# K and V loads of an attention decode step issued from GpSimd, with one packet asked for per DMA engine

## The chip, the cores and the metric

The kernel runs on one core of a Trainium2 chip. The metric is device time in microseconds (us) of one execution. The profile is one execution of the kernel as the hardware profiler records it; its span, from the first to the last instruction, is about 1.8 us shorter than the device time here.

## The reference

One decode step for four sequences: layer norm, attention over a cache of 4,096 positions with 32 heads of 192, a residual, layer norm again, and a gated feed-forward block.

```python
q = (layernorm(x) @ wq)                     # B=4, D=640 -> 32 heads x 192
scores = einsum("bhqd,bhkd->bhqk", q, k_cache) * 192 ** -0.5
o = einsum("bhqk,bhkd->bhqd", softmax(scores), v_cache)
h = x + o.reshape(B, 1, 32 * 192) @ wo
out = h + (silu(layernorm(h) @ w_gate) * (layernorm(h) @ w_up)) @ w_down
```

The K and V caches are 402.65 MB of the 424.29 MB that are read, all in bf16. Every byte is used once.

## The kernel before

The work is cut into 32 units, four heads of one sequence each. A unit needs one K tile and one V tile of 128 rows (partitions) x 49,152 bytes, 6.29 MB. There are two K slots, one V slot, and the last V goes into a free K slot. `wq` (128 rows of 61,440 bytes) shares memory with the second K slot and with V, so the second K and the first V must wait until `wq` has been used. In each unit VectorE forms four products of K and q, TensorE and VectorE sum them into scores, ScalarE takes exponentials, and TensorE forms the weighted sum of V (`pv`), one unit late.

All large loads are issued from SyncE (`sp`), in one queue:

```python
wq_land = dma("sp", lambda e: e.dma_start(wqsb..., wq...), S_wq)      # first DMA of the queue
...
def load_k(u):
    deps = [lambda: tk["tt", u - 2, NQ - 1]] if u >= 2 else ([wq_used] if u == 1 else [])
    landed["k", u] = dma("sp", lambda e: e.dma_start(
        kslot[u % 2][:, :, :].rearrange("q t d -> q (t d)"), src(kc, u)), S_k[u % 2], deps)

def load_v(u):
    if u < NU - 1:
        deps = [(lambda: tk["pv", u - 1]) if u >= 1 else wq_used]
    else:
        deps = [lambda: tk["tt", u - 1, NQ - 1]]
    landed["v", u] = dma("sp", lambda e: e.dma_start(vsrc(u)..., src(vc, u)), ..., deps)

load_k(0); load_k(1)
for u in range(NU):
    load_v(u)
    if u + 2 < NU:
        load_k(u + 2)
...   # wo in two parts (the first waits for the weighted sum of unit 30), then w_gate, w_up, w_down: all "sp"
```

`("tt", u, 3)` is the last product of unit u, `("pv", u)` the weighted sum. In a unit the fourth product is issued, then the weighted sum of the unit before. GpSimd (`pool`) only builds constants in the first 5.5 us. x is loaded from ScalarE's queue.

## Time and profile before

| | before |
|---|---|
| device time, median (range) of the first 4 runs | 989.79 us (989.71 to 990.20) |
| bytes read | 424.29 MB |
| first large DMA packet starts, last one ends (packet records) | 1.77 us, 984.75 us |
| VectorE, TensorE busy | 56%, 59% |

The first view is the page of the kernel before: the span, the busy tenths of the DMA engines and the GB/s that they moved in 40 equal slices, the queue with its packets, MB and share of 16 engines' time, the chain of work that ended last by engine, VectorE's products (busy us, mean ns | idle us before them and what ended it), and DMA issues (count, KB each, median us from issue to landing).

```profile
span 988.1 us, 9499 instructions
...
DMA  9999999999999999999999999999999999999997
GB/s 401 428 438 430 434 434 426 442 428 436 432 428 442 428 436 432 428 442 426 438 432 428 442 422 440 434 428 442 422 440 434 428 442 420 442 434 428 442 429 330
...
q1 hardware_dynamic: 10528, 424.29, 99.5%
...
DMA 67%; PE 18%; DVE 13%; issue 1%; SPq 1%; DVEq 0%
...
L412 DVE TENSOR_TENSOR prod<-k,qball 128x6144 f16<-128x6144 bf16 x128 | 426.4, 3352 | 221.1 <-DMA k<-in_A_k_cache_dram 221.1
...
k<-in_A_k_cache_dram SPq DMA_DIRECT2D x32, 6144.0 KB, 39.5
v<-in_A_v_cache_dram SPq DMA_DIRECT2D x31, 6144.0 KB, 25.5
wq_sb<-in_A_wq_dram SPq DMA_DIRECT2D x1, 7680.0 KB, 21.5
k<-in_A_v_cache_dram SPq DMA_DIRECT2D x1, 6144.0 KB, 39.5
```

The DMA engines are busy in all of the span but its last slice. The chain is two thirds DMA. VectorE sits idle 221 us for K. So the span is the stream of bytes, plus what comes before its first byte and after its last. A V lands 25.5 us after its issue, though its own transfer needs 14.5 (6.29 MB at the 433 GB/s that moved between 100 and 900 us): by that estimate about 11 us of earlier work is still queued at each issue. That is the slack an issuer has.

The second view is the timeline of the same kernel (start us, duration us, engine and line, operation; in brackets the idle time before and what ended it): the start, two pairs of issues in the steady part, and the end.

```profile
0.74 0.41 SPq L330 DMA_DIRECT2D wq_sb<-in_A_wq_dram  x1
...
22.36 0.49 PE L337 MATMUL pb<-wq_sb,lnT 128*4 128x384 bf16 x4 [12.08 <-DMA wq_sb<-in_A_wq_dram]
...
36.85 6.63 DVE L412 TENSOR_TENSOR prod<-k,qball 128x6144 f16<-128x6144 bf16 x2 [24.73 <-DMA k<-in_A_k_cache_dram]
...
855.15 0.33 SPq L365 DMA_DIRECT2D v<-in_A_v_cache_dram  x1
...
855.53 0.43 SPq L354 DMA_DIRECT2D k<-in_A_k_cache_dram  x1
...
883.35 0.33 SPq L365 DMA_DIRECT2D v<-in_A_v_cache_dram  x1
...
883.72 0.43 SPq L354 DMA_DIRECT2D k<-in_A_k_cache_dram  x1
...
941.43 3.01 SPq L376 DMA_DIRECT2D wo_sb<-in_A_wo_dram  x2
...
953.12 5.03 PE L462 MATMUL pb<-k,pbuf 128*8 128x384 bf16 x64 [3.50 <-DMA k<-in_A_v_cache_dram]
...
966.85 5.67 PE L504 MATMUL pb<-wo_sb,OT 128*4 128x160 bf16 x192 [6.50 <-DMA wo_sb<-in_A_wo_dram]
...
985.99 0.67 SPq L586 DMA_DIRECT2D out_dram<-gu  x2
```

The first product waits for the first K, 36.85 us in. V and the next K are issued together. At the end TensorE waits 3.5 us for the last V and then 6.5 us for wo.

### The profile page before, as it was taken

To read this page: it belongs to the slowest core of one execution; us is meant where nothing else is said; L and a number is where in the kernel's file an instruction comes from. 1 tells how busy PE (TensorE), PEld (TensorE's weight loads), DVE (VectorE), ACT (ScalarE), POOL (GpSimd) and SP (SyncE) were. 2 spreads that over 40 slices of the span, in tenths; PEclk is the share of its full clock that TensorE was granted. 3 is DMA by queue.
4 is the path that set the end of the run, shared out by engine and by line. 5 is a ranking of instruction groups with operands and counts; after the bars stand their busy time and mean duration, and the time that the engine had idled before them with its cause. 6 is when DMAs were issued, how large, how long until landed. Compare 5 with 4: busy or idle time off the path is not lost.

```text
span 988.1 us, 9499 instructions
## 1 busy us (share of the span) xinstructions
PE 581.9 (59%) x4422; PEld 130.3 (13%) x2955; DVE 553.4 (56%) x454; ACT 117.1 (12%) x376; POOL 3.7 (0%) x18
## 2 busy tenths in 40 slices
PE   1676454676555567556566655656665555765556
PEld 0011011111011111001111110111101011110023
DVE  2486555566655556655556665555666455566621
ACT  0311111100111110111111011111101111100120
POOL 1000000000000000000000000000000000000000
PEclk9798777887777887777788777788877778887776
DMA  9999999999999999999999999999999999999997
GB/s 401 428 438 430 434 434 426 442 428 436 432 428 442 428 436 432 428 442 426 438 432 428 442 422 440 434 428 442 422 440 434 428 442 420 442 434 428 442 429 330
DMA packets 10584, 424.40 MB, mean 430 GB/s; under 512 B 1232, under 2 KB 1232, under 8 KB 1744
## 3 DMA queue, kind: packets, MB, share of 16 engines
q1 hardware_dynamic: 10528, 424.29, 99.5%
q8 instruction: 5, 0.08, 0.0%
q14 instruction: 3, 0.02, 0.0%
q10 hardware_dynamic: 48, 0.01, 0.0%
HBM read 424.29 MB, written 0.01 MB: 429 GB/s over the span
## 4 chain that ended last, share of the span: by engine, by line
DMA 67%; PE 18%; DVE 13%; issue 1%; SPq 1%; DVEq 0%
DMA k<-in_A_k_cache_dram 64%; DVE prod L412 12%; PE pb L161 11%; PE pb L462 4%; DMA wu_sb<-in_B_w_up_dram 4%; PE pb L420 2%; SPq L365 0%; DVE sc L425 0%; PE pb L468 0%; PE pb L582 0%; DVEq L412 0%; DVE guT L576 0%; PE pb L569 0%; PE pb L560 0%; DVE gu L575 0%
## 5 line engine op out<-in xcount | busy, mean ns | idle before, releaser
L412 DVE TENSOR_TENSOR prod<-k,qball 128x6144 f16<-128x6144 bf16 x128 | 426.4, 3352 | 221.1 <-DMA k<-in_A_k_cache_dram 221.1
L161 PE MATMUL pb<-prod,identH 128*128 128x512 f16 x1408 | 384.1, 430 | 0.0
L420 PE MATMUL pb<-prod,identH 128*128 128x512 f16 x128 | 58.1, 454 | 339.9 <-DVE prod L412 339.9
L425 DVE TENSOR_REDUCE sc<-pb 128x32 f32<-128x512 f32 x128 | 88.1, 688 | 106.9 <-PE pb L161 106.9
L477 ACT ACTIVATE otmp<-pb,minv 128x192 f32<-128x192 f32 x32 | 13.4, 420 | 650.9 <-PE pb L462 650.9
L420 PEld LDWEIGHTS pb<-prod,identH 128*128 128x128 f16 x128 | 13.2, 103 | 585.9 <-DVE prod L412 485.1
L462 PE MATMUL pb<-v,pbuf 128*8 128x384 bf16 x1984 | 86.0, 326 | 0.0
L453 ACT ACTIVATE pbuf<-sc,negM 32x128 bf16<-32x128 f32 x128 | 73.4, 574 | 4.9
L462 PEld LDWEIGHTS pb<-v,pbuf 128*8 128x8 bf16 x1984 | 45.5, 87 | 28.8
L481 DVE SCALAR_TENSOR_TENSOR orow<-pb,minv,otmp 128x192 f32<-128x192 f32 x32 | 13.4, 418 | 55.2 <-ACT otmp L477 55.2
L497 PEld LDWEIGHTS pb<-orow,here 128*128 128x128 f32 x256 | 33.6, 192 | 73.5 <-issue 71.1
L497 PE MATMUL pb<-orow,here 128*128 128x48 f32 x256 | 31.7, 267 | 1.1 <-DVE orow L481 1.1
L453 ACT ACTIVATION_READ_ACCUMULATOR pbuf<-sc,negM 32x1 f32 x128 | 31.7, 248 | 0.0
L447 ACT ACTIVATE negM<-pb 128x4 f32<-128x4 f32 x32 | 5.5, 173 | 160.6 <-PE pb L443 160.6
L468 PEld LDWEIGHTS pb<-lsb,headm 128*128 128x128 f32 x64 | 12.3, 194 | 74.7 <-issue 71.1
L443 PE MATMUL pb<-negMc,ones_row 1*128 1x4 f32 x64 | 12.2, 258 | 11.9 <-DVE negMc L438 11.9
L434 PE MATMUL pb<-identF,msb 128*1 128x128 f32 x64 | 12.1, 271 | 9.8 <-DVE msb L430 9.8
L438 DVE TENSOR_REDUCE negMc<-pb 1x4 f32<-1x128 f32 x32 | 8.9, 279 | 15.1 <-PE pb L434 15.1
L443 PEld LDWEIGHTS pb<-negMc,ones_row 1*128 1x128 f32 x64 | 9.4, 183 | 21.3 <-DVE negMc L438 21.3
L468 PE MATMUL pb<-lsb,headm 128*128 128x1 f32 x64 | 9.2, 214 | 2.7 <-ACT pbuf L453 2.7
L490 ACT ACTIVATE here<-place 128x131 f32 (+1 forms) x32 | 10.0, 312 | 0.8
L430 DVE TENSOR_REDUCE msb<-sc 128x1 f32<-128x128 f32 x32 | 9.2, 286 | 1.1
(70 smaller groups left out, 89.2 us busy)
## 6 DMA issues: line engine op xcount, KB each, us to landing
k<-in_A_k_cache_dram SPq DMA_DIRECT2D x32, 6144.0 KB, 39.5
v<-in_A_v_cache_dram SPq DMA_DIRECT2D x31, 6144.0 KB, 25.5
wq_sb<-in_A_wq_dram SPq DMA_DIRECT2D x1, 7680.0 KB, 21.5
k<-in_A_v_cache_dram SPq DMA_DIRECT2D x1, 6144.0 KB, 39.5
wo_sb<-in_A_wo_dram SPq DMA_DIRECT2D x1, 5760.0 KB, 25.3
wo_sb<-in_A_wo_dram SPq DMA_DIRECT2D x1, 1920.0 KB, 27.2
wg_sb<-in_B_w_gate_dram SPq DMA_DIRECT2D x1, 1920.0 KB, 31.4
wu_sb<-in_B_w_up_dram SPq DMA_DIRECT2D x1, 1152.0 KB, 33.8
```

The costliest lines, as they stand in the source:

```text
L161: return e.add_instruction(mybir.InstMatmult(name=e.bass.get_next_instruction_name(), engine=mybir.EngineType.PE, start_tensor_calc=start, ...
L412: op("dve", lambda e: e.tensor_tensor(out=prod[BUF[k]][:, :, :], in0=kslot[u % 2][:, k * QT:(k + 1) * QT, :], in1=qball[:, bass.ds(u + pr. ...
L420: op("pe", lambda e, j=j: (e.matmul if j == 0 else partial(held_matmul, e))(psR[k][:, 0:QT * R], lhsT=identH[:, :], rhs=prod[BUF[k]][:, :, ...
L425: op("dve", lambda e: e.tensor_reduce(sc[u % 2][:, k * QT:(k + 1) * QT], psR[k][:, 0:QT * R].rearrange("q (t r) -> q t r", r=R), AX.X, ALU ...
L434: op("pe", lambda e: e.matmul(psS[0:1, XT], lhsT=msb[:, 0:1], rhs=identF[:, :], start=True, stop=True), [g("rmax", u), g("negM", u - 1), p ...
L443: op("pe", lambda e: e.matmul(psS[:, XB], lhsT=ones_row[0:1, :], rhs=negMc[0:1, :], start=True, stop=True), [g("hmax", u), g("negM", u - 1 ...
L453: op("act", lambda e, h=h, r=r: e.activation(out=pbuf[r, :, h], in_=sc[u % 2][r, :], func=ACTF.Exp, bias=negM[r, h:h + 1], scale=alpha, ac ...
L462: op("pe", lambda e, t=t, n=n: e.matmul(psO[32 * n:32 * n + 8, 0:2 * DH], lhsT=pbuf[:, t:t + 2, :].rearrange("q t m -> q (t m)"), rhs=vsrc ...
L468: op("pe", lambda e: e.matmul(psS[:, XL], lhsT=headm[:, :, :].rearrange("q r m -> q (r m)"), rhs=lsb[:, :], start=True, stop=True), [g("ex ...
L477: op("act", lambda e: e.activation(out=otmp[:, :], in_=psO[:, 0:DH], func=ACTF.Copy, scale=minv[:, 0:1]), [g("pv", u), g("minv", u), g("st ...
L481: op("dve", lambda e: e.scalar_tensor_tensor(out=orow[:, :], in0=psO[:, DH:2 * DH], scalar=minv[:, 1:2], in1=otmp[:, :], op0=ALU.mult, op1 ...
L497: op("pe", lambda e, i=i: e.matmul(psT[:, bass.ds(JW * at_unit(u)[0], JW)], lhsT=here[:, NI - 1 - i:NI - 1 - i + 128], rhs=orow[:, JW * i: ...
```

## The change

The intent, as the change reads: take the whole K and V stream, with wq ahead of it, off SyncE, let each DMA engine move its eight rows of a tile as one packet, and leave SyncE free for the weights that follow. The ending moves too: SyncE instead of GpSimd waits for the output, and GpSimd is drained at the end of the block.

```diff
+    wq_land = dma("pool", lambda e: e.dma_start(          # now ahead of the constants on GpSimd
+        wqsb..., wq...), S_wq)
     c1 = op("pool", lambda e: e.memset(r32[:, :], 0.0))
 ... (cut)
-    wq_land = dma("sp", lambda e: e.dma_start(wqsb..., wq...), S_wq)
 ... (cut)
-        landed["k", u] = dma("sp", lambda e: e.dma_start(
-            kslot[u % 2]..., src(kc, u)), S_k[u % 2], deps)
+        landed["k", u] = dma("pool", lambda e: e.dma_start(
+            kslot[u % 2]..., src(kc, u), single_packet=True), S_k[u % 2], deps)
 ... (cut)
-        landed["v", u] = dma("sp", lambda e: e.dma_start(
-            vsrc(u)..., src(vc, u)), ..., deps)
+        landed["v", u] = dma("pool", lambda e: e.dma_start(
+            vsrc(u)..., src(vc, u), single_packet=True), ..., deps)
 ... (cut; wo and the feed-forward weights stay on "sp")
-    with nc.Block(no_gpsimd_drain=True) as block:
-        pr.emit(block, "pool", fin[-1:])
+    with nc.Block() as block:
+        pr.emit(block, "sp", fin[-1:])
```

More of the change, by code (lines that the diff above doesn't have):

```diff
@@ L271, in build_kernel @@
     xd = dma("act", lambda e: e.dma_start(x16[:, :], x[:, 0, :].rearrange("b (n d) -> (b n) d", n=4)), S_x)
+    wq_land = dma("pool", lambda e: e.dma_start(
+        wqsb[:, :, :].rearrange("q c n -> q (c n)"), wq[:, :].rearrange("(q c) n -> q (c n)", c=CD)), S_wq)
     c1 = op("pool", lambda e: e.memset(r32[:, :], 0.0))
@@ L327, in build_kernel @@
     ln1 = layer_norm(psH[:, 0:DQ], [xs])
-    wq_land = dma("sp", lambda e: e.dma_start(
-        wqsb[:, :, :].rearrange("q c n -> q (c n)"), wq[:, :].rearrange("(q c) n -> q (c n)", c=CD)), S_wq)
     qcopy = []
@@ L353, in load_k @@
         deps = [lambda: tk["tt", u - 2, NQ - 1]] if u >= 2 else ([wq_used] if u == 1 else [])
-        landed["k", u] = dma("sp", lambda e: e.dma_start(
-            kslot[u % 2][:, :, :].rearrange("q t d -> q (t d)"), src(kc, u)), S_k[u % 2], deps)
+        landed["k", u] = dma("pool", lambda e: e.dma_start(
+            kslot[u % 2][:, :, :].rearrange("q t d -> q (t d)"), src(kc, u), single_packet=True), S_k[u % 2], deps)
     def vsrc(u):
@@ L364, in load_v @@
             deps = [lambda: tk["tt", u - 1, NQ - 1]]
-        landed["v", u] = dma("sp", lambda e: e.dma_start(
-            vsrc(u)[:, :, :].rearrange("q t d -> q (t d)"), src(vc, u)), S_v if u < NU - 1 else sem("s_vlast"), deps)
+        landed["v", u] = dma("pool", lambda e: e.dma_start(
+            vsrc(u)[:, :, :].rearrange("q t d -> q (t d)"), src(vc, u), single_packet=True), S_v if u < NU - 1 else sem("s_vlast"), deps)
     load_k(0)
```

## The prediction

> **What bounds the kernel now.** The DMA stream. The slice table has DMA at 9 in 39 of 40 slices; the queue table gives SyncE's queue 99.5% of all 16 engines' time. The chain of waits is 64% "DMA k". VectorE is 56% busy, TensorE 59%; the waits list has VectorE idle 221 us for K. The timeline shows SyncE issuing V and the next K in pairs, 29.04 us apart on average, right after the weighted sum of the unit before. Such a V lands 25.5 us after its issue although 6.29 MB need about 14.5 us, so about 11 us of queued work is left at each issue.
>
> **How far from its limit.** The DMA packet records show a 49,152-byte row as one packet of 1.820 us, 15,360 bytes as 0.578 us: 36.75 ns per 1,000 bytes, and some 13 ns that do not grow with size. Per transfer an engine spends 29.04/2 = 14.52 us on eight rows; by the slope alone it would be 14.45 us. The difference, 0.07 us, times 64 is 4.4 us (an estimate): all that packet merging can win.
>
> **What the change does.**
> 1. One packet of eight rows. Gain 0 to 4.4 us on the critical path; I take 3.5.
> 2. [...]VectorE's products (3.35 us each) could delay an issue, but the pair is issued after the unit's fourth product, when VectorE goes on to wait for K; even two products in a row, 6.7 us, fit into the 11 us of queued work. Cost about 0, apart from the first load: wq begins perhaps 0.7 us later, on the critical path.
> 3. The engines that move data stay the same: the rate is otherwise unchanged.
> 4. Weights now come on another queue than the last V. wo was issued at 941.4 us, when the last V had 11.7 us left. [...]wo follows it as before. Cost about 0.
> 5. [...]The records have instruction fetches at 60.8, 94 and 108 us, in mid-stream. Each might hold an engine up for one packet; less the 11 us of slack that is 0 to 3.5 us. I take 0.5 us in all.
> 6. Closing on SyncE and draining GpSimd: below 0.5 us.
>
> **Sum.** 989.85 - 3.5 + 0.7 + 0.5 = about 987.5; as the merging may be complete I say 987.0 us, 984.0 to 991.0. Faster by over 2%: 1%; within 2%: 95%; slower by over 2%: 4%.
>
> **What would show it.** Step 1: mid-stream GB/s up from 433.5 to 435, pairs 28.9 us apart. Step 2: VectorE's wait for K still about 220 us, V landing about 25 us after issue, no gaps in DMA; the first product at 37 to 38 us instead of 36.85. Step 4: last V's landing to the end still 35 us. Step 5: a single late unit near 60 to 110 us, if at all.
>
> **What would make it wrong.** [...]If packet boundaries cost nothing, step 1 gives 0 and the time is 990 to 991 us.

Cut from it, where marked, is what neither the profile of before nor a later run shows: how GpSimd's issues work inside, what could lock them out or slow single engines (step 2 and the last paragraph), why wo would follow the last V (step 4), and how long others wait for a long packet (step 5). The sum: 989.85 - 3.5 + 0.7 + 0.5 = 987.55. The 0.7 us of step 2 and the limit of 0.5 us of step 6 were guesses; experiments and profile below measure them. The 3.5 us in step 5 are an estimate, the 14.52 us of eight rows less the 11 us of slack; that a fetch waits that long was not shown. The packet records show only that each fetch in mid-stream (three in before, four in after) starts 3 to 4 ns before the record of a row ends.

## The result, and the profile after

The kernel after takes 991.20 us (median of 4 runs, 990.54 to 991.54) against 989.79 us. The ratio is 1.0013, with a 95% interval from 0.9995 to 1.0030: no difference by the 2% rule. Ratios here are the mean time of one kernel's fast runs over that of the other's fast runs of the same rounds, so they are not quite the ratio of the medians. The measured median lies 0.2 us above the predicted range, and 4.2 us above the predicted value.

The page of the kernel after, the lines that answer to those of before, with the added line of GpSimd's issues:

```profile
span 988.7 us, 9496 instructions
...
DMA  9999999999999999999999999999999999999997
GB/s 383 443 422 436 434 428 443 426 433 439 424 441 428 432 441 424 439 432 428 441 426 438 432 428 443 426 435 432 428 445 424 435 435 428 441 424 435 439 432 328
...
q0 software_dynamic: 9360, 410.52, 96.2%
q1 hardware_dynamic: 1168, 13.77, 3.3%
...
DMA 66%; PE 18%; DVE 12%; issue 2%; POOL 1%; SPq 0%; DVEq 0%; POOLq 0%
...
L412 DVE TENSOR_TENSOR prod<-k,qball 128x6144 f16<-128x6144 bf16 x128 | 426.4, 3351 | 222.8 <-DMA k<-in_A_k_cache_dram 222.8
...
L365 POOL DMA_DIRECT2D v<-in_A_v_cache_dram x31 | 16.4, 530 | 828.4 <-PE pb L462 828.4
...
k<-in_A_k_cache_dram POOLq DMA_DIRECT2D x32, 6144.0 KB, 39.0
v<-in_A_v_cache_dram POOLq DMA_DIRECT2D x31, 6144.0 KB, 25.2
wq_sb<-in_A_wq_dram POOLq DMA_DIRECT2D x1, 7680.0 KB, 21.3
k<-in_A_v_cache_dram POOLq DMA_DIRECT2D x1, 6144.0 KB, 46.4
```

The stream moved to the queue that the page calls software (q0), SyncE's queue kept 13.77 MB, and GpSimd is busy 0.53 us per issue. The packets of the two queues, 9,360 and 1,168, add up to the 10,528 of before, so the profile shows none joined. VectorE's products, its wait for K (222.8 us) and V's time to landing (25.2 us) are as before. The new thing is the last V: 46.4 instead of 39.5 us from issue to landing.

The timeline of the kernel after, same places:

```profile
1.27 0.66 POOL L273 DMA_DIRECT2D wq_sb<-in_A_wq_dram  x1 [0.81 <-POOLq L628]
...
22.73 0.49 PE L337 MATMUL pb<-wq_sb,lnT 128*4 128x384 bf16 x4 [15.88 <-DMA wq_sb<-in_A_wq_dram]
...
37.22 6.63 DVE L412 TENSOR_TENSOR prod<-k,qball 128x6144 f16<-128x6144 bf16 x2 [28.52 <-DMA k<-in_A_k_cache_dram]
...
855.43 0.53 POOL L365 DMA_DIRECT2D v<-in_A_v_cache_dram  x1 [27.21 <-PE pb L462]
...
855.95 0.53 POOL L354 DMA_DIRECT2D k<-in_A_k_cache_dram  x1
...
885.30 0.53 POOL L365 DMA_DIRECT2D v<-in_A_v_cache_dram  x1 [28.82 <-PE pb L462]
...
885.82 0.53 POOL L354 DMA_DIRECT2D k<-in_A_k_cache_dram  x1
...
943.12 3.03 SPq L376 DMA_DIRECT2D wo_sb<-in_A_wo_dram  x2
...
960.52 4.46 PE L462 MATMUL pb<-k,pbuf 128*8 128x384 bf16 x64 [9.20 <-DMA k<-in_A_v_cache_dram]
...
967.63 5.32 PE L504 MATMUL pb<-wo_sb,OT 128*4 128x160 bf16 x192 [0.45 <-DVE OT L551]
...
986.60 0.67 SPq L586 DMA_DIRECT2D out_dram<-gu  x2
```

wq is issued 0.53 us later (1.27 instead of 0.74); its first use and the first product come 0.37 us later. At the end wo is issued 1.69 us later and the weighted sum of the last V starts 7.4 us later. TensorE now waits 9.2 us for that V, but then only 0.45 us before the wo products, which start 0.78 us later than before; the output is issued 0.61 us later.

The most telling comparison comes from the DMA packet records: add up the bytes over all engines and ask at which time each kernel had moved how much. (Packets' bytes are spread evenly over their recorded time; us from the start of the span.)

```
 MB moved   before    after          wq first packet: before 1.77, after 2.63
      1.0     5.21     5.93  +0.72
     12.0    30.63    31.35  +0.71
     50.0   118.50   119.20  +0.70
    200.0   464.97   465.66  +0.69
    400.0   926.95   927.67  +0.72
    418.0   968.67   969.38  +0.71
    424.0   983.08   983.76  +0.67
```

From 50 to 400 MB both kernels take 808.5 us, 432.9 GB/s. In the profiled executions, then, the whole loss is there after the first megabyte and neither grows nor shrinks afterwards. The predicted gain along the way is absent, and so is any cost along the way. A row of 49,152 bytes is one record of 1.820 us (median) in both kernels: there are still 8,192 of them, not 1,024.

### The profile page after: what moved, and what is told of

The parts are those of the page before. It is cut to its first block, busy times and chain, and to the rows that moved or that the text cites. A ratio compares the mean times of both kernels' runs of the same rounds, so it can differ in the third digit from the quotient of the medians.

```text
span 988.7 us, 9496 instructions
## 1 busy us (share of the span) xinstructions
PE 582.4 (59%) x4422; PEld 128.8 (13%) x2955; DVE 553.4 (56%) x454; ACT 117.2 (12%) x376; POOL 37.9 (4%) x83
## 3 DMA queue, kind: packets, MB, share of 16 engines
q0 software_dynamic: 9360, 410.52, 96.2%
q1 hardware_dynamic: 1168, 13.77, 3.3%
## 4 chain that ended last, share of the span: by engine, by line
DMA 66%; PE 18%; DVE 12%; issue 2%; POOL 1%; SPq 0%; DVEq 0%; POOLq 0%
DMA k<-in_A_k_cache_dram 62%; DVE prod L412 12%; PE pb L161 12%; PE pb L462 4%; DMA wd_sb<-in_B_w_down_dram 4%; PE pb L420 2%; POOL v L365 1%; DVE sc L425 0%; PE pb L468 0%; DVEq L412 0%; POOL headm L286 0%; POOL r L277 0%; SPq L385 0%; SPq L391 0%; POOL wq_sb L273 0%
## 5 line engine op out<-in xcount | busy, mean ns | idle before, releaser
L412 DVE TENSOR_TENSOR prod<-k,qball 128x6144 f16<-128x6144 bf16 x128 | 426.4, 3351 | 222.8 <-DMA k<-in_A_k_cache_dram 222.8
L365 POOL DMA_DIRECT2D v<-in_A_v_cache_dram x31 | 16.4, 530 | 828.4 <-PE pb L462 828.4
L354 POOL DMA_DIRECT2D k<-in_A_k_cache_dram x32 | 17.0, 531 | 45.9 <-DVE prod L412 25.4
L337 PE MATMUL pb<-wq_sb,lnT 128*4 128x384 bf16 x20 | 2.1, 405 | 15.9 <-DMA wq_sb<-in_A_wq_dram 15.9
## 6 DMA issues: line engine op xcount, KB each, us to landing
v<-in_A_v_cache_dram POOLq DMA_DIRECT2D x31, 6144.0 KB, 25.2
k<-in_A_v_cache_dram POOLq DMA_DIRECT2D x1, 6144.0 KB, 46.4
```

The costliest lines, as they stand in the source:

```text
L354: landed["k", u] = dma("pool", lambda e: e.dma_start(kslot[u % 2][:, :, :].rearrange("q t d -> q (t d)"), src(kc, u), single_packet=True), ...
L365: landed["v", u] = dma("pool", lambda e: e.dma_start(vsrc(u)[:, :, :].rearrange("q t d -> q (t d)"), src(vc, u), single_packet=True), S_v ...
L412: op("dve", lambda e: e.tensor_tensor(out=prod[BUF[k]][:, :, :], in0=kslot[u % 2][:, k * QT:(k + 1) * QT, :], in1=qball[:, bass.ds(u + pr. ...
```

## The experiments

Two theories were set against each other (C to L come with the experiments that they belong to). **A**: the request for one packet changes nothing that the engines do, and the loss is the later first packet. **B**: merging does gain about 3.5 us, and the software queue loses as much somewhere. Experiments below are differences to the kernel before or after, as the diff says. Each was correct against the reference. The time of before is the median.

### 1. The request taken off the kernel after

```diff
-            kslot[u % 2]..., src(kc, u), single_packet=True), ...
+            kslot[u % 2]..., src(kc, u)), ...          # and V alike
```

> The kernel after, with the request for one packet taken off all K and V loads. Theory A (the request changes nothing that the engines do): 990.5 to 991.6 us as the kernel after, rows of 1.820 us, the last V again landing about 46 us after its issue with wo rows between its rows. Rival B (merging does gain about 3.5 us and the software queue takes as much away): 994 to 995.5 us.

Measured: 991.16 us (5 runs, 990.63 to 991.32; before 989.95), ratio 1.0011 (0.9997 to 1.0024). The last V landed 46.6 us after its issue. The same as after in time, in the rows (1.82 us each) and in the landing of the last V: A, not B.

### 2. The request alone, added to the kernel before

```diff
-            kslot[u % 2]..., src(kc, u)), ...
+            kslot[u % 2]..., src(kc, u), single_packet=True), ...     # still dma("sp"); V alike
```

> The kernel before, K and V on SyncE as before, only the request for one packet added. Theory A: 989.5 to 990.3 us, rows still 1.820 us, as before. Rival B: 985.5 to 987 us, since the gain comes without the software queue.

Measured: 989.82 us (989.76 to 989.90; before 989.95), ratio 0.9997 (0.9984 to 1.0011); rows of 1.820 us. No gain on SyncE's queue either. B is refuted from both sides.

### 3. wq alone back on SyncE

```diff
-    wq_land = dma("pool", ...
+    wq_land = dma("sp", ...          # K and V stay on "pool"
```

> The kernel after with wq alone back on SyncE. Theory C (the loss is the later first packet, 2.63 us after the start against 1.77): first packet near 1.8 us and 989.9 to 990.6 us. Rival D (the software queue costs something all along the stream): 990.8 to 991.5 us even though the first packet is early.

Measured: 996.33 us (995.99 to 997.46; before 989.95), ratio 1.0065. Both expectations missed, by about 5 us or more, and the miss taught the most. The first packet did start at 1.78 us. But the first K now stands in another queue, is issued while wq is on its way, and its transfer runs beside wq's. wq was issued at 0.75 us and took 32.2 us to land, instead of 21.5 in before, though no fewer bytes moved (432 GB/s from 15 to 35 us, 413 in before). The timeline:

```profile
33.13 0.49 PE L337 MATMUL pb<-wq_sb,lnT 128*4 128x384 bf16 x4 [22.78 <-DMA wq_sb<-in_A_wq_dram]
...
39.58 0.53 POOL L354 DMA_DIRECT2D k<-in_A_k_cache_dram  x1 [33.49 <-PE pb L161]
40.10 0.53 POOL L365 DMA_DIRECT2D v<-in_A_v_cache_dram  x1
...
41.54 6.63 DVE L412 TENSOR_TENSOR prod<-k,qball 128x6144 f16<-128x6144 bf16 x2 [29.35 <-ACT qball L404]
```

TensorE starts on wq at 33.13 instead of 22.36 us. Only when wq has been used may the second K and the first V be issued (39.58 instead of 27.9 us), and by then nothing is left in the queue: the packet records have no row starting between 36 and 39 us, and from 35 to 45 us the DMA engines are busy 0.44 of the time at 157 GB/s (before: 457 GB/s). So the order between wq and the first K, which the one queue of before kept (the last wq row starts at 19.50 us, the first row of K at 20.48), is worth about 6 us (6.4 us of time against before, 5.1 against after). Moving wq along with K and V was a necessary part of this change.

### 4. All weights into the same queue

```diff
-        t = dma("sp", lambda e, lo=lo, hi=hi: e.dma_start(wosb...      # and w_gate, w_up, w_down
+        t = dma("pool", lambda e, lo=lo, hi=hi: e.dma_start(wosb...
```

> The kernel after with wo and the feed-forward weights on GpSimd too, so that all loads stand in one queue again. Theory E (wo between the rows of the last V delays V by 6 us but not the end): the last V lands about 40 us after its issue, the time stays at 990.7 to 991.5 us. Rival F (the late V costs part of the loss): 990.0 to 990.6 us.

Measured: 991.49 us (991.11 to 991.54; before 989.95). The last V landed 39.7 us after its issue, as in before, and TensorE waited 2.5 us for V and then 7.2 us for wo, much as in before (3.5 and 6.5). The time did not improve. So the alternation of V and wo in the kernel after is real (50 of wo's 128 long rows start before V's last row, against 3 in before), and costs nothing there: the end needs both, and the sum of their bytes is the same. E, not F.

### 5 and 6. Short pieces on SyncE, without and with the request

The rows have few boundaries, so a small gain could hide. Each row is therefore cut into pieces.

```diff
+            kslot[u % 2]..., src(kc, u), max_dma_last_dim=4096), ...                      # 5
+            kslot[u % 2]..., src(kc, u), single_packet=True, max_dma_last_dim=4096), ...  # 6
```

> The kernel before with each row of K and V moved as six pieces of 8,192 bytes. The cost per piece that does not grow with size, 8 to 13 ns by the packet records, now comes five more times per row: 512 rows per engine x 5 x 8 to 13 ns = 20 to 33 us more, so 1,010 to 1,023 us. If such a cost overlaps with the transfer instead: 990 us.

> The same with the request for one packet. Theory A (the request changes nothing that these engines do with plain rows): the same as without the request within 1 us. Rival G (it merges pieces, and gained nothing in the change only because rows of 49,152 bytes have too few boundaries): back near 990 to 995 us.

The option counts bytes, not elements as the first expectation assumed: the records show pieces of 4,096 bytes, twelve to a row. Without the request: 1,043.06 us (1,042.64 to 1,043.36; before 990.12); with it 1,042.85 us (1,042.64 to 1,043.08). The page's GB/s in 40 slices and its packet counts, first without and then with the request:

```profile
GB/s 384 409 410 409 409 410 409 410 410 410 409 410 409 410 410 410 410 409 409 410 409 409 410 410 410 409 410 410 410 409 410 409 410 410 410 409 410 409 434 338
DMA packets 100696, 424.40 MB, mean 408 GB/s; under 512 B 1232, under 2 KB 1232, under 8 KB 100048
```

```profile
GB/s 385 410 409 409 409 410 410 410 410 409 410 410 409 410 410 409 410 409 410 410 409 410 410 409 410 410 409 410 409 410 410 409 410 410 409 410 410 410 431 339
DMA packets 100697, 424.40 MB, mean 408 GB/s; under 512 B 1233, under 2 KB 1233, under 8 KB 100049
```

The two agree: medians 0.2 us apart, the same packets but one. The added 52.9 us over 512 rows per engine x 11 more pieces is 9.4 ns per piece, inside the 8 to 13 ns that the expectation took from the records. So the cost per piece is real here, and the request takes none of it away. If a boundary between rows costs what one inside a row does (an estimate, not tested), the rows themselves pay 512 x 9.4 ns = 4.8 us: the 4.4 us of the prediction was then right as a size and wrong as something to be won this way.

### 7 and 8. The same pieces on GpSimd, with and without the request

```diff
+            kslot[u % 2]..., src(kc, u), single_packet=True, max_dma_last_dim=4096), ...  # 7, "pool"
+            kslot[u % 2]..., src(kc, u), max_dma_last_dim=4096), ...                      # 8, "pool"
```

> The kernel after (GpSimd, one packet asked for) with the same pieces of 8,192 bytes. Theory A: about 1 us above the run without the request on SyncE, as the queues differ by that alone; records still of single pieces. Rival G: near 991 to 996 us. Rival H (software pays for each piece): GpSimd busy per issue well above 0.53 us and more than 10 us above the SyncE run.

> GpSimd with pieces of 4,096 bytes, without the request for one packet (its run with the request: 1,062.4 us, GpSimd 1.01 us per issue, the last V 70.6 us from issue to landing because wo rows of 46,080 bytes alternate with its pieces). Theory A: the same within 2 us, the same 70 us. Rival G (the request merges at least in the software queue): a different tail or rate, over 5 us apart.

Measured: 1,062.44 us (1,061.31 to 1,064.38) with, 1,064.74 us (two runs, 1,063.74 and 1,065.75) without. Their ranges overlap; the medians are 2.3 us apart, slightly more than the 2 us allowed, with two runs on one side, and the last V landed 71.5 us after its issue without the request and 70.6 with it. G, over 5 us apart, fails. The expectation of 1 us over SyncE was missed by 18 us. Both signs of H did come (GpSimd busy 1.01 us per issue, 19 us over SyncE), but its cause, that software pays for each piece, does not account for the loss. It is not the rate: by the progress of bytes the run with the request is 1.0 us behind the SyncE run at 50 and at 400 MB. It is the end, in the timeline of the run with the request:

```profile
995.06 3.03 SPq L376 DMA_DIRECT2D wo_sb<-in_A_wo_dram  x2
...
1036.20 4.80 PE L462 MATMUL pb<-k,pbuf 128*8 128x384 bf16 x64 [33.05 <-DMA k<-in_A_v_cache_dram]
...
1043.65 4.93 PEld L504 LDWEIGHTS pb<-wo_sb,OT 128*4 128x4 bf16 x192 [0.57 <-DVE OT L551]
```

The last V, issued at 965.61 us, landed 70.6 us later, and TensorE waited 33 us for it with wo long there. Between 1,000 and 1,005 us the records hold 48 V pieces of 4,096 bytes and 48 wo rows of 46,080: linked from the end of one to the start of the next, they stand one piece, one row, one piece on nearly every engine. So here the engines took one packet from each queue in turn, 4,096 bytes of V for 46,080 of wo, and V got a twelfth of the bytes. Had eight rows (96 pieces) been one packet, the records would not show wo rows between single pieces. This is direct evidence that there is no merged packet of that kind, and it shows what the alternation of experiment 4 can cost when one queue's packets are small.

### 9. The first DMA of the kernel before held back

```diff
-    wq_land = dma("sp", ..., S_wq)
+    wq_land = dma("sp", ..., S_wq, [c2])        # c2: GpSimd has made the identity
```

> The kernel before, wq on SyncE held back until GpSimd has made the identity (about 3.1 us after the start; it was issued at 0.74). Theory C (a later first packet costs its delay in full): first packet near 4.1 instead of 1.77 us and 992.0 to 992.6 us. If other slack took the delay up: 990 us.

Measured: 992.39 us (992.14 to 992.86; before 990.12). The first packet started at 4.13 instead of 1.77 us, 2.36 us late. The progress of bytes is 2.1 to 2.2 us late from the first to the last megabyte, and the means differ by 2.34 us. Here the late first packet was paid in full.

### 10. wq and the first K on SyncE, everything else as after

```diff
-    wq_land = dma("pool", ...
+    wq_land = dma("sp", ...
-        landed["k", u] = dma("pool", ...
+        landed["k", u] = dma("pool" if u else "sp", ...       # with its own semaphore for u == 0
-    ... ([wq_used] if u == 1 else [])
+    ... ([lambda: qbc[-3]] if u == 1 else [])                 # K(1) only when K(0) has nearly landed
```

> The kernel after with wq and the first K both on SyncE, in one queue and in the order of before; all later K and V stay on GpSimd, the second K issued only when the first K has nearly landed, so that the queues hardly overlap. Theory C (the late first packet is nearly all of the loss): first packet near 1.8 us, 989.8 to 990.5 us. Rival D (the software queue costs about 1 us along the stream): 990.8 to 991.5 us.

Measured: 992.16 us (991.82 to 992.38; before 990.14), slower than after and above both expected ranges. Read by the time alone, this would speak against C. The timeline and the records say otherwise:

```profile
0.75 0.41 SPq L273 DMA_DIRECT2D wq_sb<-in_A_wq_dram  x1
...
35.02 0.67 POOL L354 DMA_DIRECT2D k<-in_A_k_cache_dram  x1 [29.54 <-ACT qball L404]
...
36.72 6.63 DVE L412 TENSOR_TENSOR prod<-k,qball 128x6144 f16<-128x6144 bf16 x2 [24.57 <-DMA k<-in_A_k_cache_dram]
```

The stream is 0.07 us ahead of before up to 14 MB, as theory C has it, falls back by 2.0 us between 14 and 20 MB, and stays at 1.9 us to the end. The fall is the hand-over from SyncE to GpSimd: the records have 1.1 us per engine without a packet around 36 us, and the rows of K and V take 0.9 us more per engine in sum; why was not shown. So GpSimd's queue itself lost nothing over 400 MB here, but the experiment brought a loss of its own and its time doesn't confirm C.

### 11. The ending of before

```diff
-    with nc.Block() as block:
-        pr.emit(block, "sp", fin[-1:])
+    with nc.Block(no_gpsimd_drain=True) as block:
+        pr.emit(block, "pool", fin[-1:])
```

> The kernel after with the ending of before (GpSimd waits for the output, no drain of GpSimd). If the new ending costs nothing: 990.8 to 991.5 us. If it costs the part of the loss that the late first packet leaves: 990.3 to 990.7 us.

Measured: 990.98 us (990.63 to 991.28; before 990.14). Within the scatter of the kernel after: the new ending has no cost that these runs can show.

### 12 and 13. An issue from GpSimd while VectorE forms a product

```diff
-            if k == NQ - 1 and u >= 1:      # weighted sum of the unit before, after the fourth product
+            if k == 1 and u >= 1:           # 12: after the second
...
-        deps = [(lambda: tk["pv", u - 1]) if u >= 1 else wq_used]
+        deps = [lambda: tk["pv", u - 1], lambda: tk["rsum", u, 1]] if u >= 1 else [wq_used]   # 13
```

> The kernel after with the weighted sum of the unit before taken up after the second product instead of the fourth, so that GpSimd issues V while VectorE is in its products of 3.35 us. Theory L[...]: the V issues last up to 3.9 us instead of 0.53, or the products get longer; time within 1 us of the kernel after, as the queue holds more than that. Rival: 0.53 us for every issue.

> As the run with the early weighted sum, whose V issues turned out to fall between products; here V also waits for the second row sum, right after which VectorE starts its fourth product, so that the issue falls into a product. Theory L[...]: V issues of up to 3.9 us instead of 0.53, or products that get longer; the time stays within 1 us of the kernel after, as the queue holds 11 us of work. Rival: 0.53 us as everywhere.

Experiment 12 missed its purpose: 990.61 us (two runs), but no issue fell into a product. In 13 thirty issues did. Its time is 991.14 us (990.82 to 991.87; before 990.16). One unit in its timeline:

```profile
221.27 3.35 DVE L412 TENSOR_TENSOR prod<-k,qball 128x6144 f16<-128x6144 bf16 x1
221.65 0.53 POOL L365 DMA_DIRECT2D v<-in_A_v_cache_dram  x1 [26.11 <-DVE sc L425]
```

The issue at 221.65 us lies inside the product that starts at 221.27. All thirty took 0.527 to 0.530 us, and the products' median stayed at 3.349 us (3.350 in after). No sign of theory L, of longer issues or longer products. What is seen is the time of the issue on GpSimd and the time of landing (20.8 us, now issued earlier); the stream stays 0.85 us behind before from 50 to 400 MB, so it was not held up either. A delay of a few us between an issue and its first packet would not show: 20.8 us less the 14.5 of the transfer leaves about 6 us of queued work, by the same estimate as before.

### 14. The kernel after once more

> The kernel after once more, unchanged, on the same chip as its rounds of before. If the loss is the 0.7 us by which its stream runs late plus the scatter of runs: 0.5 to 1.3 us over before. If there is more to it: over 1.3 us again and again, with a profile in which the stream falls back along its way.

Measured: 990.91 us (990.56 to 991.16; before 990.16), means 0.79 us apart; its stream is 0.76 us late at 1 MB and 0.77 at 418 MB.

| kernel | mean minus mean of before | runs |
|---|---|---|
| after, first rounds | +1.25 us | 4 and 4 |
| after without the request (1) | +0.98 us | 5 and 9 |
| after with the old ending (11) | +0.83 us | 5 and 9 |
| after again (14) | +0.79 us | 5 and 9 |

The other runs that keep the stream on GpSimd in one piece lie 1.30 (experiment 4), 0.48 (12, two runs) and 1.14 us (13) above before. The loss in the table is 0.8 to 1.25 us; 0.7 to 0.8 us of it is the late stream. The rest, up to half a microsecond, is as large as the scatter of before itself (989.65 to 990.49) and could not be placed.

No version was found that beats both kernels. The stream is full from its first packet to its last in both (DMA at 9 in 39 of 40 slices), and the experiments only offer ways to start it later or to break its order.

## Why the prediction was wrong

- **Bound by the stream of bytes: right.** DMA at 9 in 39 slices before and after, 432.9 GB/s in both, VectorE's wait for K 221 and 223 us.
- **Step 1, "One packet of eight rows. Gain 0 to 4.4 us on the critical path; I take 3.5": this is the step that failed.** It measured 0. The request changes nothing: not on GpSimd (1), not on SyncE (2), not with twelve times the boundaries (5 and 6), and in the turn-taking with wo the packets are single pieces (7). The size of the prize was well estimated (9.4 ns per piece, and 4.8 us in all by the estimate of experiment 5); what was argued and never shown was that the request removes it. Why the request changes nothing, whether it is dropped on the way or the engines ignore it, no run shows. Leaving out the 3.5 us gives 991.05 us by the same sum; 991.20 was measured. That the two are so close is partly luck: the sum still holds the 0.5 us of step 5, which did not occur, and up to 0.5 us of the measured loss could not be placed. The upper end of the range, 991.0, was the "gives 0" case with nothing added for scatter. The repeat in experiment 14, 990.91 us, falls inside the range, so the 0.2 us by which the result lies outside it is within the scatter; the gain that did not come is what failed. The lower end, 984.0, had no term behind it: the full 4.4 us with step 2's 0.7 us gives 986.2.
- **Step 2, the issues moved to GpSimd, "Cost about 0, apart from the first load": right.** The 0.7 us for the first load measured 0.7 us by progress of bytes (0.86 by the first packet: 0.53 of later issue, 0.33 of longer time from issue to packet, 1.36 instead of 1.03), and in experiment 9 a delay of 2.36 us was paid in full. No cost afterwards. The reason given, that the issues avoid the products, holds as a fact in the trace of after (none of GpSimd's 65 issues falls into a product), but was not needed: issues inside products took the same time (13, 0.527 to 0.530 us).
- **Step 3, unchanged rate: right**, 808.5 us for 350 MB in both.
- **Step 4, "wo follows it as before": wrong.** V and wo alternate packet by packet (experiment 4) and V lands 6.9 us later after its issue. Its cost was still about 0, as predicted, for another reason: TensorE's former wait for wo (6.5 us) turned into a longer wait for V (9.2 instead of 3.5 us). No more than that was spare, since wo's products then started 0.45 us after the weighted sum was ready; experiment 7 shows the cost when V comes later still.
- **Step 5, an engine held up for one long packet, 0.5 us: no such cost.** Packets are no longer than before (1.820 us), so its ground is gone too.
- **Step 6, ending below 0.5 us: right** as far as the scatter lets one see (11).

## What to carry to other kernels

In this kernel, whose DMA queue never runs dry, moving the stream to another issuing engine changed only its ends. To see such a thing, compare the bytes moved against time: a constant offset from the first megabyte on says at once that the start, and not the rate, is what changed. One queue was also an order here: what must land first (wq, 6 us) or must not be starved (the last V, some 18 us with small pieces) did best in one queue ahead of its rivals. Holding the rivals back in another queue instead had a cost of its own, 2 us in experiment 10. Before a cost per packet is booked as a gain, count the packets in a profile with the option on.
